# The lead-in of a fused attention and GLU block: weight loads on one queue, the first copy ahead of the second Sqrt, two more tiles transposed by DMA, paced loads

## The chip, the cores and the metric

The kernel runs on one core of a Trainium2 chip. The metric is the device time of one execution in microseconds (us); several executions are timed and the median is quoted. All points in time inside an execution are counted from the start of the profile's span (its first instruction). "Granted clock" is the mean clock that TensorE was allowed, 1.0 being full.

## The reference

The input x has 2048 rows of 640 numbers (bf16). The parts that matter here:

```python
xn  = (x - mean(x)) / sqrt(var(x) + 1e-5)          # LN, row by row
qkv = xn @ wqkv                                    # 640 x 1920
o   = sliding_dilated_attention(q, k, v)           # 32 heads of 20, window 8, dilation 2
out = x + o @ wo + ((xn @ w_gate) * (xn @ w_up)) @ w_down
```

The kernel cuts the rows into 16 tiles of 128. Each tile is loaded, normalised on VectorE, and transposed, because TensorE needs xn with the 640 columns on the partitions. The projections to q and k then run tile by tile for tiles 0 to 3 (128-column matmuls), in pairs of tiles for 4 to 7 (256 columns: the "wide" projections), and four tiles at a time from tile 8 on (512 columns). After that TensorE has nothing but long runs of 512- and 320-column matmuls until the end.

## The kernel before

Every operation is recorded in program order by a small scheduler, which puts it on its engine's list and inserts the semaphore waits. So the order of the Python calls is the order on each engine.

The loads. SyncE ("sp") and ScalarE ("act") share the weights of q (group 0) and k (group 1):

```python
x_load(1, "act")
x_load(0)
for c in range(NCH):                     # NCH = 5 chunks of 128 rows
    wqkv_load(0, c, ("sp", "act")[c % 2])
x_load(2, "act")
x_load(3)
for c in range(NCH):
    wqkv_load(1, c, ("sp", "act")[c % 2])
for t in range(4, 8):
    x_load(t)
```

LN of one tile is spread over four helpers. Tiles 0 to 3 are transposed on TensorE (`ln_pe`) and copied out of PSUM (`ln_copy`); tiles 4 to 15 (`NTP = 4`) go through a DMA transpose on SyncE's queue, and each applied tile sends for the x eight tiles ahead:

```python
def ln_aggr(t):
    ...                                  # bn_aggr on VectorE
    if t >= 8:                           # 1/sqrt on GpSimd: an addition, then pow(-0.5)
        ...
        return
    op("act", ... ACT.Sqrt ...)          # on ScalarE; VectorE takes the reciprocal

def ln_apply(t):
    ...
    op("dve", ... (x - mean) * rstd ...)
    if t >= NTP:
        op("sp", lambda e: e.dma_start_transpose(o, xs), ...)
    if t + 8 < NT:
        x_load(t + 8)
    elif t == NT - 1:
        late_loads()

def ln_next(t):
    ln_stats_b(t); ln_aggr(t); ln_stats_a(t + 1); ln_apply(t)
```

Note the last function: VectorE takes half of the statistics of tile t+1 *before* it applies tile t. A late x of tile 5 therefore holds back tile 4.

## Time and profile before

| | before |
|---|---|
| median time | 255.28 us (3 runs, 255.06 to 255.30) |
| span of the profile | 253.7 us |
| TensorE busy | 249.7 us, 98% |
| first projection / tile 2 / wide / 512 columns start at | 6.72 / 13.98 / 19.57 / 30.48 us |
| DMA transposes of tiles 5, 7, 11 land at | 18.79, 22.95, 29.93 us |

Two lines of the profile page, from its parts 1 and 4 (busy time with its share of the span and the number of instructions; shares of the chain of work that ended last):

```profile
PE 249.7 (98%) x1573; PEld 149.3 (59%) x1573; DVE 216.5 (85%) x241; ACT 112.9 (45%) x202; POOL 47.0 (19%) x73
...
PE 95%; DMA 2%; DVE 1%; ACTq 0%; ACT 0%; issue 0%
```

TensorE (PE) is the bound, and all but about the first ten and the last two microseconds of the chain are its own work. The timeline of TensorE, from 5 to 40 us (columns: start, duration, engine, source line, operation, output<-inputs, shapes, count, and in brackets the idle time before and what ended it):

```profile
6.72 1.03 PE L468 MATMUL PS<-XNT,WQKV 128*128 128x128 bf16 x15 [0.18 <-ACT XNT L414]
...
10.34 0.45 PE L403 MATMUL PS<-IDENT,XNS 128*128 128x128 bf16 x5 [0.34 <-DVE XNS L389]
...
13.98 5.75 PE L457 MATMUL PS<-XNT,WQKV 128*128 128x128 bf16 x100
19.57 11.08 PE L475 MATMUL PS<-XNT,WQKV 128*128 128x256 bf16 x100
30.48 9.88 PE L442 MATMUL PS<-XNT,WQKV 128*128 128x512 bf16 x45
```

L403 is a transpose on TensorE, the others are projections. After 10.34 us no bracket stands on any of these lines: TensorE never waits again. So whatever it gains or loses before about 31 us goes into the span in full.

The timeline of SyncE's DMA queue in the same stretch. A line is the time that the queue was held by the issue of a transfer, not the transfer itself:

```profile
13.94 1.33 SPq L393 DMA_TRANSPOSE XNT<-XNS  x1
15.32 0.57 SPq L294 DMA_DIRECT2D XST<-in_A_x_dram  x1
15.93 1.21 SPq L393 DMA_TRANSPOSE XNT<-XNS  x1
...
21.44 0.58 SPq L294 DMA_DIRECT2D XST<-in_A_x_dram  x1
22.07 14.79 SPq L393 DMA_TRANSPOSE XNT<-XNS  x8
```

The issue of a transpose holds the queue for 1.21 us, that of an x load for 0.58. The queue has only four loads between its transposes and then eight transposes in a row, with pauses, as they wait for VectorE. Tile 11's lands at 29.93, and TensorE wants it at 30.48: the slack is 0.55 us. Tile 5's is 0.8 us, tile 7's about 2 us.

### The profile page before, as it was taken

What the parts mean: (1) busy time and instruction counts of PE and PEld (TensorE: products, weight loads), DVE (VectorE), ACT (ScalarE), POOL (GpSimd) and SP (SyncE); (2) the same over time, 40 slices, a digit from 0 to 9 for tenths busy, and PEclk for the clock granted to TensorE, in tenths of its full rate; (3) what the DMA queues carried; (4) which work ended last, traced back from release to release, by engine and by line L of the source; (5) the groups of instructions that cost most, each with busy time, mean ns of one, the idle gap of its engine ahead of it and who ended that gap; (6) DMA issues with size and microseconds to landing.
All of it is one profiled execution on the core that took longest, in us unless ns stands there. A gap on an engine that the chain in (4) does not pass through costs nothing.

```text
span 253.7 us, 3853 instructions
## 1 busy us (share of the span) xinstructions
PE 249.7 (98%) x1573; PEld 149.3 (59%) x1573; DVE 216.5 (85%) x241; ACT 112.9 (45%) x202; POOL 47.0 (19%) x73
## 2 busy tenths in 40 slices
PE   8999999999999999999999999999999999999996
PEld 3899955555554444444444447764444777777775
DVE  5896679999999994999999994899999999995221
ACT  3575557555555557555555553325555112211000
POOL 2003320113453252002232102120000112112000
PEclk9999999999999999999999999999999999999999
DMA  6959448967866546364469962393000042332311
GB/s 213 332 117 170 82 79 303 375 178 142 138 127 110 106 83 125 114 238 90 75 117 253 393 230 24 51 314 68 3 0 0 4 50 26 36 45 26 80 52 52
DMA packets 25665, 31.84 MB, mean 126 GB/s; under 512 B 10000, under 2 KB 22160, under 8 KB 25616
## 3 DMA queue, kind: packets, MB, share of 16 engines
q1 hardware_dynamic: 18448, 21.31, 26.7%
q0 software_dynamic: 6336, 9.31, 23.7%
q10 hardware_dynamic: 864, 0.98, 1.2%
q8 instruction: 12, 0.20, 0.3%
q14 instruction: 5, 0.04, 0.0%
HBM read 14.42 MB, written 4.59 MB: 75 GB/s over the span
## 4 chain that ended last, share of the span: by engine, by line
PE 95%; DMA 2%; DVE 1%; ACTq 0%; ACT 0%; issue 0%
PE PS L614 41%; PE PS L645 29%; PE PS L442 17%; PE PS L475 4%; PE PS L457 2%; DMA XST<-in_A_x_dram 2%; PE PS L468 1%; DVE STATS L358 0%; ACTq L294 0%; PE PS L403 0%; ACT L321 0%; DVE XNS L389 0%; DVE STATS L364 0%; DVE FOUT L654 0%; DVE MV L370 0%
## 5 line engine op out<-in xcount | busy, mean ns | idle before, releaser
L614 PE MATMUL PS<-XNT,WG 128*128 128x512 bf16 x240 | 59.6, 379 | 0.0
L614 PE MATMUL PS<-XNT,WU 128*128 128x512 bf16 x240 | 59.6, 379 | 0.0
L581 DVE TENSOR_TENSOR PVB<-VO,ATB 128x10240 f16<-128x10240 bf16 x8 | 43.9, 5489 | 0.2
L442 PE MATMUL PS<-XNT,WQKV 128*128 128x512 bf16 x200 | 43.3, 379 | 0.0
L645 PE MATMUL PS<-WD,HT 128*128 128x320 bf16 (+1 forms) x300 | 43.2, 294 | 0.0
L614 PEld LDWEIGHTS PS<-XNT,WU 128*128 128x128 bf16 x240 | 23.5, 98 | 28.3
L614 PEld LDWEIGHTS PS<-XNT,WG 128*128 128x128 bf16 x240 | 23.5, 98 | 28.2
L616 ACT ACTIVATE USX<-PS 128x512 bf16<-128x512 f32 x48 | 28.7, 597 | 22.6 <-PE PS L614 22.2
L645 PEld LDWEIGHTS PS<-WD,HT 128*128 128x128 bf16 x300 | 28.7, 98 | 10.9
L442 PEld LDWEIGHTS PS<-XNT,WQKV 128*128 128x128 bf16 x200 | 23.5, 118 | 19.4
L576 DVE TENSOR_TENSOR PVB<-PVB 128x5120 f16<-128x5120 f16 (+1 forms) x16 | 34.5, 2156 | 0.3
L509 POOL DMA_DIRECT2D LOG<-PE x24 | 22.5, 937 | 57.6 <-DMA LOG<-PE 57.4
L649 ACT ACTIVATE FACC<-PS 128x320 f16<-128x320 f32 x24 | 10.5, 437 | 41.9 <-PE PS L645 41.9
L616 ACT ACTIVATE HT<-PS 128x512 bf16<-128x512 f32 x36 | 21.5, 597 | 16.5 <-PE PS L614 16.5
L645 PE MATMUL PS<-WO,VO 128*128 128x320 bf16 (+1 forms) x165 | 27.1, 295 | 0.0
L660 POOL DMA_DIRECT2D out_dram<-FACC x12 | 10.4, 865 | 71.2 <-ACT FACC L649 71.2
L645 PEld LDWEIGHTS PS<-WO,VO 128*128 128x128 bf16 x165 | 15.9, 98 | 5.9
L498 DVE TENSOR_TENSOR TMP<-QH,KH 128x2048 f16<-128x2048 bf16 x16 | 19.1, 1218 | 0.0
L498 DVE TENSOR_TENSOR PP<-QH,KH 128x2048 f16<-128x2048 bf16 x16 | 18.9, 1218 | 0.0
L503 DVE TENSOR_TENSOR PP<-PP,TMP 128x4096 f16<-128x4096 f16 x8 | 18.3, 2291 | 0.2
L654 DVE TENSOR_TENSOR FOUT<-PS,XR 128x320 bf16<-128x320 f32 (+1 forms) x9 | 4.1, 455 | 15.8 <-PE PS L645 15.8
L449 ACT ACTIVATE VO<-PS 128x512 bf16<-128x512 f32 x20 | 11.9, 597 | 9.6 <-PE PS L442 9.6
(65 smaller groups left out, 227.8 us busy)
## 6 DMA issues: line engine op xcount, KB each, us to landing
PE<-PP POOLq DMA_DIRECT2D x8, 512.0 KB, 4.8
ATB<-LOG SPq DMA_DIRECT2D x8, 512.0 KB, 4.3
LOG<-PE POOLq DMA_DIRECT2D x24, 128.0 KB, 2.7
XST<-in_A_x_dram SPq DMA_DIRECT2D x14, 160.0 KB, 4.7
WG<-in_B_w_gate_dram SPq DMA_DIRECT2D x1, 1920.0 KB, 9.4
WU<-in_B_w_up_dram SPq DMA_DIRECT2D x1, 1920.0 KB, 16.1
WD<-in_B_w_down_dram SPq DMA_DIRECT2D x1, 1920.0 KB, 10.3
out_dram<-in_A_x_dram SPq DMA_DIRECT2D x1, 1920.0 KB, 10.1
```

The costliest lines, as they stand in the source:

```text
L442: op("pe", (lambda l, x, c: lambda e: e.matmul(PS[:, b, :], l, x, start=(c == 0), stop=(c == NCH - 1)))(l, x, c), r=[l, x], w=[PS[:, b, :] ...
L449: op("act", lambda e: e.activation(o, PS[:, b, :], ACT.Copy, scale=sc), r=[PS[:, b, :]], w=[o], name=f"pev{which}_{m}_{j}")
L498: return (1.22, lambda: op("dve", lambda e: e.tensor_tensor(o, qw, kw, ALU.mult), r=[q, k], w=[o], name=f"prod{h}_{p}_{c}"))
L503: (2.3, lambda: op("dve", lambda e: e.tensor_tensor(a, a, b, ALU.add), r=[a, b], w=[a], name=f"psum{h}_{p}")),
L509: op("pool", lambda e: e.dma_start(o, i, accum_op=ALU.add), r=[o, i], w=[o], dma=True, name=name)
L576: return lambda: op("dve", lambda e: e.tensor_tensor(o, x, y, ALU.add), r=[x, y], w=[o], name=f"{name}_{b}")
L581: lambda: op("dve", lambda e: e.tensor_tensor(PVB[:], vw, aw, ALU.mult), r=[v, a], w=[PVB[:]], name=f"pv_{b}")),
L614: op("pe", (lambda l, x, c: lambda e: e.matmul(PS[:, b, :], l, x, start=(c == 0), stop=(c == NCH - 1)))(l, x, c), r=[l, x], w=[PS[:, b, :] ...
L616: op("act", lambda e: e.activation(o, PS[:, b, :], ACT.Copy), r=[PS[:, b, :]], w=[o], name=f"guev{which}_{m}_{j}")
L645: op("pe", (lambda l, x, i, b: lambda e: e.matmul(PS[:, b, 0:wid], l, x, start=(i == 0), stop=(i == n - 1)))(l, x, i, b), r=[l, x], w=[PS[ ...
L649: op("act", (lambda o, b: lambda e: e.activation(o, PS[:, b, 0:wid], ACT.Copy))(o, b), r=[PS[:, b, :]], w=[o], name=f"fin{t}_{nb}")
L660: stores.append(op("pool", lambda e: e.dma_start(d, f, accum_op=ALU.add), r=[f, ("out",)], w=[("out", t)], dma=True, name=f"oacc{t}"))
```

## The change

The intent: start TensorE sooner and take work off it. The weights go to one queue, so that all loads come in one order and x2 lands earlier (before: at 7.93 us). The copy of tile 0 goes ahead of the second Sqrt on ScalarE. Tiles 2 and 3 are transposed by DMA, so TensorE is spared ten transposes. To keep their DMA transposes from queueing behind x loads, the loads are paced: only x0 to x4 go out at the start, the others after the transposes. Both projections of one tile run together, so that tile 3 is wanted later. Not in the title, but in the diff: 1/sqrt of tiles 8 to 15 goes from GpSimd to ScalarE.

```diff
-    NTP = 4
+    NTP = 2
@@ the loads
     for c in range(NCH):
-        wqkv_load(0, c, ("sp", "act")[c % 2])
-    x_load(2, "act")
+        wqkv_load(0, c)
+    x_load(2)
     x_load(3)
     for c in range(NCH):
-        wqkv_load(1, c, ("sp", "act")[c % 2])
-    for t in range(4, 8):
-        x_load(t)
+        wqkv_load(1, c)
+    x_load(4)
@@ ln_aggr, ln_apply
-        if t >= 8:
-            (1/sqrt on GpSimd: cut)
-            return
...
-        if t + 8 < NT:
-            x_load(t + 8)
-        elif t == NT - 1:
+        ahead = {2: (5, 6), 3: (7, 8)}.get(t, (t + 5,) if t > 3 else ())
+        for u in ahead:
+            if u < NT:
+                x_load(u)
+        if t == NT - 1:
             late_loads()
@@ the lead-in
     ln_pe(0)
+    ln_copy(0, "act")
     ln_stats_b(1)
     ln_aggr(1)
-    ln_copy(0)
+    ln_copy(0, "dve")
@@ tr(t)
-        ln_pe(t)
-        ln_copy(t)
+        if t < NTP:
+            ln_pe(t)
+            ln_copy(t)
@@ the projections of tiles 0 to 3
-        for which in (0, 1):
-            for t in (t0, t0 + 1):
+        for which, t in ((0, 0), (0, 1), (1, 0), (1, 1)) if t0 == 0 else ((0, 2), (1, 2), (0, 3), (1, 3)):
...
-                    at = {(0, 0): (3, lambda: tr(1)), (0, 1): (4, lambda: tr(2)), (1, 1): (2, lambda: tr(3))}
+                    at = {(0, 0): (4, lambda: tr(1)), (1, 0): (3, lambda: tr(2)), (1, 1): (4, lambda: tr(3))}
```

More of the change, by code (lines that the diff above doesn't have):

```diff
@@ L284, in build_kernel @@
     EPSC = sb("EPSC", [128, 16], FP32)
-    NEGH = sb("NEGH", [128, 16], FP32)
     IDENT = sb("IDENT", [128, 128])
@@ L304, in build_kernel @@
     op("pool", lambda e: e.memset(VO[:, :, 0:VP], 0.0), w=[VO[:, :, 0:VP]], name="vpad")
-    op("pool", lambda e: e.memset(NEGH[:], -0.5), w=[NEGH[:]], name="negh")
     op("pool", lambda e: e.memset(MASK[:], 0.0), w=[MASK[:]], name="mask0")
@@ L370, in ln_aggr @@
         op("dve", lambda e: e.bn_aggr(mv, st), r=[st, ("stb", t)], w=[mv], name=f"bnag{t}")
-        if t >= 8:
-            rstd = SD[:, t, 1:2]
-            op("pool", lambda e: e.tensor_scalar(sd, mv[:, 1:2], EPS, None, op0=ALU.add), r=[mv], w=[("sd", t)], name=f"sd{t}")
-            op("pool", lambda e: e.tensor_tensor(rstd, sd, NEGH[:, 0:1], ALU.pow), r=[("sd", t), NEGH[:]], w=[("rstd", t)],
-               name=f"rstd{t}")
-            return
         op("act", lambda e: e.activation(sd, mv[:, 1:2], ACT.Sqrt, bias=EPSC[:, 0:1]), r=[mv, EPSC[:]], w=[("sd", t)],
@@ L384, in ln_apply @@
         sd, rstd = SD[:, t, 0:1], SD[:, t, 1:2]
-        if t < 8:
-            op("dve", lambda e: e.reciprocal(rstd, sd), r=[("sd", t)], w=[("rstd", t)], name=f"rstd{t}")
+        op("dve", lambda e: e.reciprocal(rstd, sd), r=[("sd", t)], w=[("rstd", t)], name=f"rstd{t}")
         for c0, c1 in ((0, 2 * 128), (2 * 128, D)) if t == 0 else ((0, D),):
@@ L403, in ln_pe, with ln_copy @@
             op("pe", (lambda o, i: lambda e: e.transpose(o, i, IDENT[:]))(o, i), r=[i, IDENT[:]], w=[o], name=f"tr{t}_{c}")
-    def ln_copy(t):
+    def ln_copy(t, only=None):
         parts = ((("act", 0, 2), ("dve", 2, NCH)), (("dve", 0, 2), ("act", 2, NCH)), (("act", 0, NCH),),
@@ L408, in ln_copy @@
         for eng, c0, c1 in parts:
+            if only is not None and eng != only:
+                continue
             o = XNT[:, c0:c1, t * TS:(t + 1) * TS]
@@ L709, in build_kernel @@
             bank_ring[:] = [5, 6, 0, 7, 2, 3, 4, 1]
-        for which in (0, 1):
-            for t in (t0, t0 + 1):
+        for which, t in ((0, 0), (0, 1), (1, 0), (1, 1)) if t0 == 0 else ((0, 2), (1, 2), (0, 3), (1, 3)):
+            if True:
                 b = bank()
```

## The prediction

> **What bounds the kernel now.** TensorE. On the profile page it is busy 249.7 of 253.7 us (98%), and 95% of the chain that ended last is its own. The timeline shows no gap in its matmuls from 10.34 us to 251.4 us, so only the lead-in can change the time: an advance there that still stands when the wide projections (pairs of tiles) start at 19.57 us, and the 512-column ones at 30.48 us, passes through whole.
>
> **What is to be won, by the timeline.**
> - The first copy of tile 0 waits on ScalarE behind the second Sqrt (6.10, copy at 6.30), though its two transposes were done near 5.5. Moved ahead, the first projection starts when the two filler matmuls have streamed, near 6.2 instead of 6.72: 0.5 us.
> - Gap of 0.26 us at 8.69 (copy behind tile 2's statistics; x2 landed at 7.93) and of 0.5 us before 10.34. With all loads in one order x2 is eighth. Loads landed every 0.5 to 0.58 us in this trace, so about 6.5 to 7.1. The Trainium skill, "DMA: Bandwidth & Descriptors" (Issuing engines are not separate DMA queues), says that several issuers only save sequencer time; here SyncE issues one load per 0.45 us, about the landing rate, so I expect no loss of bandwidth.
> - Ten TensorE transposes (two fives of 0.28 us issue time): 0.56 us.
>
> Projections of tiles 0 and 1 should thus end near 12.2 us instead of 13.98: about 1.75 us.
>
> **What it adds.** A DMA transpose holds SyncE's queue for 1.2 us and lands 2.6 to 4.2 us after issue. VectorE applies tile 2 at about 9.3 to 9.7, so its transpose lands at 12.4 to 13.3: a wait of 0.2 to 1 us at once. Then the paced loads: x5 goes out only after that transpose, at 11.0, and lands near 13.8 (2.8 us in this trace). VectorE runs the statistics of tile 5 before it applies tile 4, so it stands idle for some 1.5 us; the application of tile 4 moves from 13.46 to about 14.5, of tile 5 from 15.14 to 16.1. With x9 before it on the queue, tile 5's transpose is issued at 16.8 (before 15.93) and lands at 19.5 to 20.5. The wide projections need it; TensorE would be ready at 18.1 to 18.8. So it waits about 1 us and starts at 19.4 to 20.5, against 19.57. A load after every transpose (1.87 us a tile on SyncE) also puts tile 11's transpose at about 27.9, landing 30.5 to 31.2.
>
> Sqrt for tiles 8 to 15 returns to ScalarE (0.29 us, GpSimd 0.8), so LN ends 2 us sooner; nothing waits for that.
>
> **Sum.** 1.75 us is gained by the end of tile 1, and nearly all given back at tiles 2, 5 and perhaps 11. My chain gives -0.2 to +0.9 us; the latencies, read from loads under other contention, are uncertain by half a microsecond each, and a luckier x5 keeps up to 1 us of gain. I say 255.2 us, range 254.2 to 256.3. Faster by over 2%: 1%, within: 98%, slower: 1%.
>
> **What would show it.** Right: first projection near 6.2, tile 1 done near 12.2, TensorE idle before tile 2's and above all before the first wide projection, put down to a DMA transpose; VectorE idle near 12 to 14 waiting for x. Wrong on the cost: wide projections start near 18 us and the time is near 253.7. Wrong on the gain: x2 still lands near 8.
>
> **What would make it wrong.** Transposes queued behind loads landing over 4 us late; late K weights; the idle time lowering the granted clock; qk products starting earlier and colliding with the weight loads.

## The result, and the profile after

The change is slower, by about 1.5%: 258.75 us median of 6 runs (257.68 to 260.78) against 255.22 (255.06 to 255.34). The ratio is 1.0146, with a 95% interval of 1.0107 to 1.0184. The prediction of 255.2 (254.2 to 256.3) was wrong. Note the spread too: before stays within 0.3 us, the change scatters over 3 us.

The traced execution was the fastest of the six (257.68 us, span 255.4). The same two lines of its page:

```profile
PE 248.9 (97%) x1563; PEld 148.5 (58%) x1563; DVE 217.9 (85%) x249; ACT 112.9 (44%) x208; POOL 41.1 (16%) x56
...
PE 86%; DVE 6%; DMA 4%; SPq 1%; issue 1%; ACT 0%
```

TensorE has 0.8 us less to do, but its share of the chain fell from 95% to 86%: VectorE, DMA landings and SyncE's queue are now on it. TensorE's timeline:

```profile
6.12 1.28 PE L462 MATMUL PS<-XNT,WQKV 128*128 128x128 bf16 x20
...
8.16 4.38 PE L462 MATMUL PS<-XNT,WQKV 128*128 128x128 bf16 x75 [0.20 <-DVE XNT L406]
13.26 5.78 PE L451 MATMUL PS<-XNT,WQKV 128*128 128x128 bf16 x100 [0.72 <-DMA XNT<-XNS]
19.82 5.66 PE L469 MATMUL PS<-XNT,WQKV 128*128 128x256 bf16 x50 [0.78 <-DMA XNT<-XNS]
26.23 5.65 PE L469 MATMUL PS<-XNT,WQKV 128*128 128x256 bf16 x50 [0.76 <-DMA XNT<-XNS]
32.13 8.15 PE L436 MATMUL PS<-XNT,WQKV 128*128 128x512 bf16 x37 [0.25 <-ACT SD L368]
```

The first projection starts 0.6 us earlier, and tiles 0 and 1 are done near 12.4 instead of 13.98. Then TensorE waits for DMA transposes: for tile 2, for tile 5 (first wide projection), for tile 7 (second one), and for tile 11 (its transpose landed at 32.04; the profile names the Sqrt that ended just before). The 512-column projections start at 32.13 instead of 30.48, 1.65 us later, and the span is 1.7 us longer.

SyncE's queue:

```profile
16.85 1.21 SPq L383 DMA_TRANSPOSE XNT<-XNS  x1
18.10 0.58 SPq L293 DMA_DIRECT2D XST<-in_A_x_dram  x1
18.72 2.17 SPq L383 DMA_TRANSPOSE XNT<-XNS  x1
20.94 0.58 SPq L293 DMA_DIRECT2D XST<-in_A_x_dram  x1
21.56 1.21 SPq L383 DMA_TRANSPOSE XNT<-XNS  x1
...
28.53 0.58 SPq L293 DMA_DIRECT2D XST<-in_A_x_dram  x1
29.15 7.40 SPq L383 DMA_TRANSPOSE XNT<-XNS  x5
```

Load and transpose now take turns up to tile 11, 1.87 us a tile (1.21 and 0.58, and two pauses of 0.04), without a break. One transpose, tile 6's, held the queue for 2.17 us. Tile 11's goes out at 29.15 (before: 27.30) and lands at 32.04 (before: 29.93).

Two more traces of the same kernel were taken later (runs e13 and e14). The starts, in us:

| | before | after | e13 | e14 |
|---|---|---|---|---|
| first projection | 6.72 | 6.12 | 6.04 | 6.04 |
| tile 2 | 13.98 | 13.26 | 13.34 | 13.47 |
| first wide | 19.57 | 19.82 | 20.32 | 19.84 |
| tile 11's transpose issued / landed | 27.30 / 29.93 | 29.15 / 32.04 | 29.44 / 32.37 | 29.30 / 32.28 |
| 512 columns | 30.48 | 32.13 | 32.68 | 32.59 |
| span | 253.7 | 255.4 | 255.7 | 255.6 |
| time minus span | 1.83 | 2.28 | 2.28 | 2.32 |

So e13 and e14 show the same loss as the first trace; they did not catch one of the slower runs, for which they were taken. The last row of the table is a surprise of its own: 0.46 us of the difference lies outside the profile's span. It is taken up by e16 to e18.

### The profile page after: what moved, and what is told of

It reads as the page before. It is cut to its first block, busy times and chain, and to the rows that moved or that the text cites. A ratio compares the mean times of both kernels' runs of the same rounds, so it can differ in the third digit from the quotient of the medians.

```text
span 255.4 us, 3830 instructions
## 1 busy us (share of the span) xinstructions
PE 248.9 (97%) x1563; PEld 148.5 (58%) x1563; DVE 217.9 (85%) x249; ACT 112.9 (44%) x208; POOL 41.1 (16%) x56
## 4 chain that ended last, share of the span: by engine, by line
PE 86%; DVE 6%; DMA 4%; SPq 1%; issue 1%; ACT 0%
PE PS L608 41%; PE PS L639 29%; PE PS L436 17%; DMA XST<-in_A_x_dram 4%; DVE STATS L361 2%; DVE XNS L379 2%; DVE STATS L355 2%; SPq L293 1%; DVE MV L367 1%; DVE SD L376 1%; SPq L383 0%; DVE FOUT L648 0%; ACT SD L368 0%; DVE XNT L406 0%
## 5 line engine op out<-in xcount | busy, mean ns | idle before, releaser
L503 POOL DMA_DIRECT2D LOG<-PE x24 | 21.7, 920 | 59.4 <-DMA LOG<-PE 59.4
L648 DVE TENSOR_TENSOR FOUT<-PS,XR 128x320 bf16<-128x320 f32 (+1 forms) x9 | 4.1, 455 | 15.5 <-PE PS L639 15.5
```

Source lines behind the costliest of these rows:

```text
L503: op("pool", lambda e: e.dma_start(o, i, accum_op=ALU.add), r=[o, i], w=[o], dma=True, name=name)
```

## The experiments

The theories. A: the paced loads, taking turns with the transposes on SyncE's queue, make the transposes of tiles 5, 7 and 11 late. B: the DMA transposes of tiles 2 and 3 are what costs. C: Sqrt of tiles 8 to 15 on ScalarE holds up the copies out of PSUM there and so TensorE. D: a long wait of TensorE cuts its clock. E: instruction fetches delay the transposes in flight. F, about the time outside the span, came late. "Before" ran beside every group, on the same chip: 255.4 to 255.7 us.

### e1 to e4: one part undone at a time

e1, only the pacing undone:

```diff
-    x_load(4)
+    for t in range(4, 8):
+        x_load(t)
...
-        ahead = {2: (5, 6), 3: (7, 8)}.get(t, (t + 5,) if t > 3 else ())
+        ahead = (t + 8,)
```

> The change with only the pacing undone: x4 to x7 go out at the start, each later load eight tiles ahead. Theory A (paced loads put tiles 5, 7 and 11 on a chain of SyncE issues and DMA landings): tile 2's transpose lands later, near 13.8 us, behind more loads, but VectorE no longer waits for x5, the first wide projection starts near 19.4 instead of 19.8 and the 512-column projections near 30.5 instead of 32.1; time 255.0 to 255.8 us. Rival B (the DMA transposes of tiles 2 and 3 are what costs): stays above 257. Rival C (Sqrt of tiles 8 to 15 on ScalarE ties LN to the PSUM copies): stays above 257.

e2, only tiles 2 and 3 back on TensorE:

```diff
-    NTP = 2
+    NTP = 4
```

> The change with only tiles 2 and 3 back on TensorE transposes. Theory A: x5 and x6 need not wait behind a transpose any more and land near 12.5, tile 2 costs TensorE no wait; first wide projection near 18.5, but SyncE still alternates load and transpose up to tile 10, so tile 11 lands near 29.6 to 30.5 and the 512-column projections start at about 29.8 to 30.6; time 254.4 to 255.4 us. Rival B: as good as before or better, 254.0 to 254.5, with no wait left on the later tiles. Rival C: above 257.

e3, both edits together:

> Both undone: left are the one queue for the weights, the earlier first copy, the order of projections and Sqrt on ScalarE throughout. Theory A: nothing holds TensorE after tile 1; 512-column projections start near 29.3, time 253.8 to 254.4 us, better than before. Rival C: above 257, as Sqrt on ScalarE is still there.

e4, the change with 1/sqrt of tiles 8 to 15 on GpSimd again (the lines of `ln_aggr` and the reciprocal's `if t < 8` of before put back):

> The change with 1/sqrt of tiles 8 to 15 back on GpSimd. Theory A: no tile 8 to 15 is limited by it, so the same as the change, 257.5 to 259.5 us, or up to 0.5 us slower, as LN needs 2.1 us a tile instead of 1.66. Rival C (ScalarE's Sqrt holds the PSUM copies and TensorE's banks): back to 255 to 256.

| | median (range), us | before beside it | ratio [95%] |
|---|---|---|---|
| e1 pacing undone | 258.82 (257.15 to 260.03) | 255.65 | 1.0121 [1.0068, 1.0174] |
| e2 tiles 2, 3 on TensorE | 256.64 (256.09 to 259.18) | 255.65 | 1.0061 [1.0009, 1.0112] |
| e3 both | 255.67 (255.29 to 256.67) | 255.65 | 1.0009 [0.9983, 1.0035] |
| e4 1/sqrt on GpSimd | 259.06 (258.65 to 262.02) | 255.65 | 1.0161 [1.0102, 1.0219] |

Theory C falls with e4: the time does not come back, not even in its two runs at a full clock (258.65 and 258.66). Theory A alone falls with e1. Without pacing, tile 2's transpose is issued at 9.97 but lands at 15.04, because five more x loads are ahead of it, and TensorE's timeline reads:

```profile
15.08 7.41 PE L452 MATMUL PS<-XNT,WQKV 128*128 128x128 bf16 x100 [2.35 <-DMA XNT<-XNS]
22.32 11.08 PE L470 MATMUL PS<-XNT,WQKV 128*128 128x256 bf16 x100
```

The wait is 2.35 us. And look at the duration: the 100 matmuls that take 5.78 us in the change take 7.41 here. The granted clock fell after the wait, to 0.50 for 3.41 us. The view by stretches shows it (the stretch and its length, busy times of the five engines, then the clock, the DMA share and GB/s):

```profile
15.51:18.92 3.41, 3.41 (x36) 3.41 (x35) 1.85 (x6) 0.78 (x2) 0.00 (x0) 0.50 0.85 188
```

Three of e1's four runs have such a cut (mean clock 0.993). The one at a full clock took 257.15 us, less than any full-clock run of the change (257.68 to 259.36), but still 1.5 us more than before. So the equal medians of e1 and the change hide two things: at a full clock undoing the pacing wins something (by one run), and the longer wait at tile 2 that it brings cuts the clock more often. The pacing does what it was made for, at tile 2, and takes away later what it gave.

e2 recovers 2.2 us of the 3.2 that separate the change (258.83 in e9) from before, and e3 all of it; neither theory had forecast e2's time, which is above both of its ranges. So B is the larger part. Once the two transposes are gone the pacing has nothing to protect, and the turns on the queue (A) are worth the other 1 us: tile 11's transpose went out at 28.99 us in e2's trace and at 26.97 in e3's. My expected gain for e3 (253.8 to 254.4) did not come. Its trace shows the 512-column projections at about the same time as before; about 0.5 us of its lead was lost waiting for tile 7, whose transpose landed at 24.85 instead of 22.95. Another half is outside the span: e3's four spans (253.0 to 254.4 us) are a little shorter than those of before beside it (253.4 to 254.2), but 2.3 us are lost outside them instead of 1.8 (see e16).

In e2's trace, its slowest run (259.18), the clock shows again:

```profile
13.35 5.75 PE L451 MATMUL PS<-XNT,WQKV 128*128 128x128 bf16 x100
21.05 12.78 PE L469 MATMUL PS<-XNT,WQKV 128*128 128x256 bf16 x100 [1.95 <-DMA XNT<-XNS]
```

The wide projections, 11.08 us at a full clock, took 12.78 after a wait of 1.95 us. The mean clock of that run is 0.993; the other three runs have 1.0 and lie at 256.1 to 256.7.

### e5: does a long wait cut the clock?

```diff
+    def filler(n):            # n matmuls of 512 zero columns into the bank that comes next
+        ...
+                if (which, t) == (0, 2):
+                    filler(4)
...
+            if g == 0:
+                filler({4: 5, 6: 4}[t0])
```

> The change, with 4, 5 and 4 filler matmuls (0.22 us each) on TensorE just before the three places where it waits for DMA transposes. Theory D (a wait of TensorE near 2 us or longer halves its clock for some us and costs another 1.6 us; that makes the upper half of the change's times): mean granted clock 1.0 in every run, the slow runs are gone, all runs 257.4 to 258.8 us, median near 258.0. Rival (the spread comes from DMA landings alone): spread as before, 257.5 to 261, median 0.3 to 0.6 us later than the change's 258.75.

Measured: 259.68 us (258.64 to 260.01), ratio 1.0154. Half a miss. The clock was 1.0 in all four runs (lowest 0.999), and the range is 1.4 us instead of 3. But the median did not fall. In its trace tile 2's transpose held the queue for 2.60 us, tile 5's landed at 22.3, and TensorE waited 1.81 us on top of the fillers. The test was not clean, though: tile 7's transpose landed at 25.26, long before TensorE wanted it, so the four fillers there (27.80 to 28.67) cost 0.87 us for nothing. Without them the trace would stand at about 258.8 (an estimate), the change's median. What settles it is the change itself: ten of its eleven runs (e9's 681 us aside) have a clock of 0.999 or 1.0, and these lie between 257.68 and 259.36. So the clock explains the highest times, not the middle.

Over all traces (without e9 and e12, see there), a wait of TensorE for a transpose was followed by slow matmuls in five of seven cases where it lasted 1.95 us or more (e1 2.35, e2 1.95, e4 2.74, e6 2.00, e7 3.77; not in e7's first, 2.00, nor in e8, 2.35), and in none where it was 1.86 us or less. Each cut lasted 3.41 us at half the clock and so cost 1.6 to 1.7 us; one such cut in some 256 us makes the mean clock of 0.993, and two make the 0.987 of the slowest runs of e4 and e8 (an estimate: neither was traced). The Trainium skill, "TensorE: Matmul & The Clock Gate" (Part 1), says that the clock falls to half after an idle window of about 3.4 us, and that this window runs freely. The traces fit this in that the same wait, 2.00 us, is punished in e6 and not in e7; but here four of the five waits that were punished lasted only 1.95 to 2.74 us, and the measurement decides.

### e6: does an instruction fetch delay the transposes?

The 2.17 us of tile 6's transpose and the landing of tile 7's, 4.6 us after its issue, had no cause in the kernel. But the DMA view has a queue of kind "instruction" with one packet near each. The DMA view of the change, narrowed to 19.0 to 19.5 us and to 24.0 to 24.5 us (queue, kind: packets, MB, share of 16 engines in that half microsecond):

```profile
q8 instruction: 1, 0.02, 16.8%
```

```profile
q14 instruction: 1, 0.01, 9.7%
```

The first packet, 16 KB, took 16.8% of 16 engines for 0.5 us: 1.34 us on one engine. To test it, the fetch was moved:

```diff
-    warm(10)                  # 10 warm-up matmuls of 512 columns
+    warm(36, 128)             # 36 of 128 columns: as long, but 52 instructions more
```

> The change, with the 10 warm-up matmuls of 512 columns replaced by 36 of 128 columns: as long, but 52 more TensorE instructions ahead, so that each later 16 KB fetch of the instruction queue comes 26 matmuls, some 1.5 to 3 us, earlier. Theory E (an instruction fetch delays the transposes in flight by 1 to 2 us): the fetch at 19.0 us moves to about 17.3, tile 5's transpose (issued 16.85) then lands near 21 to 22 instead of 19.75, tile 6's issue is no longer the long one, TensorE waits 2 us or more before the first wide projection; median 259.5 to 261 us. Rival (the long landings come from the load beside each transpose): the long ones stay at tiles 6 to 8, time as the change, 257.7 to 259.4.

Measured: 258.36 us (257.79 to 258.97), ratio 1.0111. The size was a miss, the mechanism a hit. The fetch moved from 19.10 to 16.40 us, and SyncE's queue of this run reads:

```profile
14.83 1.21 SPq L383 DMA_TRANSPOSE XNT<-XNS  x1
16.08 0.58 SPq L293 DMA_DIRECT2D XST<-in_A_x_dram  x1
16.71 2.09 SPq L383 DMA_TRANSPOSE XNT<-XNS  x1
18.84 0.58 SPq L293 DMA_DIRECT2D XST<-in_A_x_dram  x1
19.47 1.21 SPq L383 DMA_TRANSPOSE XNT<-XNS  x1
```

The long hold went from tile 6 (now the 1.21 at 19.47) to tile 5 (2.09), and the long flight, 4.4 us, to tile 4. TensorE waited 2.00 us before the first wide projection, and its clock was cut in three of the four runs. The time did not rise because the earlier fetch moved too (10.58 to 9.81), and tile 2's transpose, which it used to hit, landed at 12.4 instead of 13.2: there was no wait at tile 2.

All traces together say the same. Take the 194 DMA transposes issued after 13 us in the 16 traces whose x loads are all on hardware queues. The 93 with no instruction packet during their flight landed 2.6 to 3.3 us after issue (median 2.8). The 101 with one had a median of 3.5 and went up to 4.9; all 52 flights over 3.45 us are among them. Every transpose that held the queue for more than 1.45 us had a fetch beside it. The Trainium skill, "DMA: Bandwidth & Descriptors" (Queues, rings and completion order), says that a DMA engine takes turns between its queues packet by packet. A 16 KB packet of 0.9 to 1.9 us would then hold back whatever a transpose has queued on the same engine. That this is the way it happens is argued, not shown; and a fetch is no certain delay, as 28 of the 101 landed within 3.0 us all the same.

### e7 and e8: the x loads on GpSimd's queue

e7, the change with x9 to x15 issued by GpSimd, so that SyncE has only transposes from tile 4 on:

```diff
-                x_load(u)
+                x_load(u, "pool" if u > 8 else "sp")
```

> The change, with x9 to x15 loaded from GpSimd's queue, so that SyncE issues transposes alone from tile 4 on. Theory A (load and transpose take turns on SyncE's queue at 1.87 us a tile): tile 5's transpose is issued near 16.6, tile 7's near 20.0 instead of 21.56, tile 11's near 26.6 instead of 29.15; the waits before the second wide projection and the 512-column ones (0.95 and 0.3 us) go, the one at tile 5 stays; 256.0 to 257.4 us. If the bytes in flight and not the queue's turns are what delays them: 257.7 to 259.4.

e8, an attempt at a better kernel: e3, with x8 to x15 on GpSimd's queue and `ln_stats_a(2)` after the copy of tile 1:

> An attempt at a better kernel: early first copy, weights on one queue and projections tile by tile are kept; tiles 2 and 3 go back to TensorE, x4 to x7 go out at the start, x8 to x15 from GpSimd's queue, and the statistics of tile 2 follow the copy of tile 1 on VectorE. TensorE then waits at neither tile 1 nor tiles 5, 7, 11: first wide projection near 18.4 us, 512-column ones near 29.3 to 29.8, 254.0 to 254.8 us against 255.3 to 255.7 before. If a fetch still lands late transposes on TensorE: 255.2 to 256.2.

Both missed by far: e7 260.21 us (258.55 to 261.61), ratio 1.0180; e8 258.83 (257.50 to 262.49), ratio 1.0111; e8's 262.49 counts as a slow run, and without it the median is 258.17. The issues do come earlier (tile 7's at 20.76), but the landings do not. The DMA view of e7 for tile 7's issue alone (last column: us from issue to landing):

```profile
XNT<-XNS SPq DMA_TRANSPOSE x1, 7.1
```

Tiles 4 to 9 took 5.3, 6.5, 6.3, 7.1, 5.6 and 4.0 us; tiles 10 to 14, when the loads were over, 2.6 each. So, for the landings, loads from GpSimd's queue in flight beside a transpose are far worse than loads between the transposes on SyncE's own queue, where both land in about 2.9 us; why, these runs don't show, and ScalarE's queue was not tried. In time the difference is smaller: three of e7's four runs have a cut clock (0.993), and the fourth took 258.55 us, about as long as the change. The queue's turns were not the only price of the paced loads, but they were the cheaper way to pay it.

### e9, e13, e14: the change again

> The change itself once more, on the chip of the runs beside it, for a second trace and its spread: 257.5 to 261 us. Every theory expects the waits of TensorE at tile 2 and before the first wide projection; if an instruction fetch is what delays transposes, the transposes in flight at the fetch near 19 and near 24 us are again the ones over 3.5 us; if a wait near 2 us cuts the clock, a run with a mean clock of 0.993 has one and is over 1.5 us longer than the fastest.

> The change, one more trace, for a typical run (its first trace was its fastest run of six). If it is DMA landings behind instruction fetches that make 258.8 out of 257.7 at a full clock: one of tiles 2 to 7 lands 1 us or more later than in the first trace, with a fetch inside its flight, and TensorE's wait grows by as much; nothing after 35 us differs.

> As the run before: a third trace. The same two expectations; if the extra time is instead after the lead-in, the 512-column projections start near 32.1 us in both and the end still differs.

e9: 258.83 us (three runs of 258.29 to 258.87, ratio 1.0125); its fourth, the traced execution, took 681 us, with TensorE slow from end to end (512-column matmuls of 835 ns instead of 379), and is left aside. e13 and e14 gave 257.98 and 257.92 us. TensorE in e14:

```profile
13.47 5.78 PE L451 MATMUL PS<-XNT,WQKV 128*128 128x128 bf16 x100 [0.84 <-DMA XNT<-XNS]
19.84 11.11 PE L469 MATMUL PS<-XNT,WQKV 128*128 128x256 bf16 x100 [0.59 <-DMA XNT<-XNS]
32.59 7.72 PE L436 MATMUL PS<-XNT,WQKV 128*128 128x512 bf16 x35 [1.64 <-ACT QH L477]
```

The time is lost in the lead-in, as in the first trace, but at other places: no wait at tile 7, 1.64 us at tile 11. (That one of tiles 2 to 7 would land later and TensorE's wait there grow was expected and did not come: tile 6's landed at 23.58 instead of 22.55, but nothing waited for it.) The weight load of that first 512-column matmul started at 32.34, right after tile 11's landing at 32.28, so the transpose is what mattered; the ScalarE copy that the bracket names ended 0.1 us later. In all three traces tile 11's issue is where the sum of the queue puts it: from tile 4's at 14.97, 15.75 and 15.21, seven turns of 1.87 us give 13.1, and the rest (1.1, 0.6 and 1.0 us) is what a fetch held the queue (tile 6's transpose 0.96 over its usual time; x11's load 0.57; x11's load 0.96). In e13 a fetch had also held the queue at tile 2's transpose (2.25 us instead of 1.32), and from there its tile 4 is late.

### e10: the DMA transposes alone, on the kernel before

```diff
-    NTP = 4
+    NTP = 2
...
-        ln_pe(t)
-        ln_copy(t)
+        if t < NTP:
+            ln_pe(t)
+            ln_copy(t)
```

> The kernel before, with only tiles 2 and 3 transposed by DMA. If these transposes are what costs (theory B): tile 2's lands at 14 to 15.5 us behind x loads, TensorE waits 1 to 2.5 us before tile 2 and its clock may be cut; 256.8 to 259.5 us. If the pacing or Sqrt on ScalarE costs (A, C): within 0.5 us of before.

Measured: 256.51 us (256.10 to 259.13), ratio 1.0062 [1.0025, 1.0099]. Theory B again: this part alone costs 1 us, and 3.7 us in the one run whose clock was cut (0.993). Tile 2's transpose was issued at 10.32 and landed at 14.6, and TensorE, which had saved ten transposes, lost more than it saved:

```profile
14.64 5.78 PE L457 MATMUL PS<-XNT,WQKV 128*128 128x128 bf16 x100 [1.55 <-DMA XNT<-XNS]
```

### e11: the one queue alone, on the kernel before

```diff
-        wqkv_load(0, c, ("sp", "act")[c % 2])
-    x_load(2, "act")
+        wqkv_load(0, c)
+    x_load(2)
...
-        wqkv_load(1, c, ("sp", "act")[c % 2])
+        wqkv_load(1, c)
```

> The kernel before, with only the weights and x2 moved to SyncE's queue. x2 lands at 7.4 to 7.9 instead of 7.93; the gaps of TensorE at 8.69 and 10.34 us shrink by 0.2 to 0.6 us in all and nothing later moves: 254.7 to 255.3 us. If weights on one queue arrive later than TensorE wants them: slower, 255.5 to 256.5.

Measured: 255.08 us (255.03 to 255.37) against 255.47, ratio 0.9987 [0.9974, 1.0000]. This is the best kernel, by 0.13%: small, as expected, and just at the edge of what the runs resolve. x2 landed at 7.39 instead of 7.93:

```profile
9.83 0.45 PE L403 MATMUL PS<-IDENT,XNS 128*128 128x128 bf16 x5 [0.20 <-DVE XNS L389]
...
13.49 5.75 PE L457 MATMUL PS<-XNT,WQKV 128*128 128x128 bf16 x100
19.08 11.08 PE L475 MATMUL PS<-XNT,WQKV 128*128 128x256 bf16 x100
30.04 10.31 PE L442 MATMUL PS<-XNT,WQKV 128*128 128x512 bf16 x47
```

Half a microsecond is won at tile 2 and kept to the end. No more could be: tile 11's transpose landed at 29.95, so the slack there is now 0.1 us. The skill's word on queues, cited in the prediction, holds here roughly: the last weights of k landed at 10.43 us in the change and 10.81 in e11 with one queue, and at 10.19 with two, and the timeline shows no matmul waiting for them.

### e12, e15, e17: two more attempts at a better kernel

e12 and e15 are one kernel: e3, with `ln_stats_a(2)` after the copy of tile 1, and with the transposes of tiles 1 and 3 one chunk of five matmuls earlier in TensorE's order.

> Second attempt at a better kernel: early first copy, one queue, projections tile by tile, Sqrt on ScalarE are kept; tiles 2 and 3 on TensorE, loads eight tiles ahead, statistics of tile 2 after the copy of tile 1, tile 1's transposes after 15 matmuls. Tile 1 done near 12.9 us, first wide projection near 18.4 (19.57 before); fetches still delay tiles 6 and 7 and give back some 0.5 us: 254.6 to 255.4 us against 255.5.

> The second attempt at a better kernel once more (its trace fell into a state with a clock of 0.756): 254.9 to 257.3 us. If late landings of tiles 6 and 7 take its gain: TensorE is done with tile 1 near 12.9 us, starts the first wide projection near 18.4, and waits 0.5 to 2 us before the second.

e12: one execution of 330 us, its traced one, had a granted clock of 0.756 and is left aside; the other five lie at 254.87 to 257.25, median 256.58, ratio 1.0036 [1.0011, 1.0062]: a little slower than before, and above the 254.6 to 255.4 expected. e15: 256.48.

e17 is e3 with eight idle GpSimd instructions (see e16):

> A third attempt at a better kernel: run e3 (tiles 2 and 3 on TensorE, loads eight tiles ahead; the early copy, the one queue, the order of projections and Sqrt on ScalarE kept) with the eight idle GpSimd instructions. Theory F: the time exceeds the span by 1.8 us, so 255.2 us median (254.8 to 256.2), 0.45 us better than e3 and level with the queue-only kernel. Rival: 255.7 us as e3.

e17: 256.20 us (254.50 to 256.42), ratio 1.0017 [0.9995, 1.0039], against an expected median of 255.2. Its six runs are two groups, 254.5 and 254.9, and 256.15 to 256.42. The two traces, of two kernels that differ a little, suggest why such a kernel has two times. TensorE in e15, and then in e17's fastest run:

```profile
12.85 5.75 PE L452 MATMUL PS<-XNT,WQKV 128*128 128x128 bf16 x100
20.00 11.11 PE L470 MATMUL PS<-XNT,WQKV 128*128 128x256 bf16 x100 [1.41 <-DMA XNT<-XNS]
31.17 9.01 PE L437 MATMUL PS<-XNT,WQKV 128*128 128x512 bf16 x41
```

```profile
12.97 5.75 PE L455 MATMUL PS<-XNT,WQKV 128*128 128x128 bf16 x100
18.55 11.08 PE L473 MATMUL PS<-XNT,WQKV 128*128 128x256 bf16 x100
29.47 10.74 PE L440 MATMUL PS<-XNT,WQKV 128*128 128x512 bf16 x49
```

In both, tile 5's transpose went out at 15.5 to 15.6 us. In e15 an instruction fetch came at 17.58 and the transpose landed at 19.96; in e17 it came at 17.70 and the transpose landed at 18.25. So TensorE waits 1.41 us in the one and not in the other, for fetches that are 0.1 us apart (0.2 counted from the issue). That this small shift makes the difference is argued, not shown. The slow group of e17 was not traced itself; that it is the same event is an inference from e15.

### e16 and e18: the time outside the span

Theory F: 2.28 us instead of 1.82 outside the span comes from GpSimd having nothing to do between 2.5 and 33 us.

e16, the change with one idle GpSimd addition for each of tiles 8 to 15:

```diff
+        if t >= 8:
+            op("pool", lambda e: e.tensor_scalar(scr, mv[:, 1:2], EPS, None, op0=ALU.add), ...)
```

> The change with eight idle GpSimd instructions more (a scalar addition of 0.2 us for each of tiles 8 to 15, whose result nobody reads), between about 20 and 35 us. Of every run of a kernel in which GpSimd worked in that stretch, the time exceeds the profile's span by 1.8 us, of every run of the others by 2.28 us. Theory F (that stretch of GpSimd without work costs 0.46 us outside the span): 1.8 us here, 258.3 us instead of 258.8. Rival (it hangs on the pow, on another op or on the number of instructions, 73 against 56): 2.28 us.

e18, the change with 17 tiny memsets on GpSimd at the very start:

> The change with 17 more GpSimd instructions (tiny memsets) at the very start and none later, so that it has as many as before. Theory F (idle stretch): time minus span stays 2.28 us. Rival (number of instructions): 1.8 us. The time itself is that of the change, 257.5 to 260 us.

Both bring it back. Time minus span is 1.77 to 1.86 us in e16's four runs and 1.78 in e18. So F, the idle stretch, falls: in e18 GpSimd has nothing to do from 5.0 to 34.9 us, nearly as in the change (2.5 to 35.6). Of the explanations named, the number of GpSimd instructions is left. The change and e3 have 56 and lose 2.28; before has 73, e18 73, e16, e17 and e8 64, e7 63, and all of these lie at about 1.8 (1.75 to 1.99). Where on the way to the end this time passes, the profile does not show. In the time, e16 gave 258.17 us (257.86 to 258.78), ratio 1.0104; e18 gave 256.68 in its one run, faster than any run of the change itself, with no late tile 7 and a fetch at 18.9.

## Why the prediction was wrong, point by point

- *TensorE is the bound and only the lead-in counts.* Right. In nearly every trace the shift at 30 to 33 us is, within 0.2 us (0.4 in e10), the shift of the span.
- *First projection near 6.2, x2 at 6.5 to 7.1, tile 1 done near 12.2.* Right but for x2 (7.39): 6.12, and about 12.4.
- *A wait of 0.2 to 1 us at tile 2; the first wide projection at 19.4 to 20.5.* Right: about 0.7 to 0.8 us, and 19.8 to 20.3.
- *VectorE waits for x5.* Right: the timeline shows it idle for 1.36 us before the statistics of tile 5, until 13.91.
- *"A load after every transpose (1.87 us a tile on SyncE) also puts tile 11's transpose at about 27.9, landing 30.5 to 31.2."* This is the step that failed. The turns were sized right, 1.87 us each, and tile 5 stood where the forecast had it (16.8; 16.85 in the first trace). But the sum had no term for the queue being held: between tiles 4 and 11 the fetches add 0.6 to 1.1 us to it, and in e13 another 0.9 at tile 2. Tile 11 was issued at 29.15 to 29.44 and landed at 32.0 to 32.4. The forecast then took this tile only for a possible extra ("and perhaps 11") and summed to -0.2 to +0.9 us; the traces have +1.65 to +2.2 in the lead-in. In the first trace tile 7 was late as well (a flight of 4.62 us beside a fetch), which the forecast did not have at all.
- *The sum had no term for what lies outside the span.* The diff also takes 17 instructions off GpSimd, to which the prediction gave no cost. They are worth 0.46 us (e16, e18). Together with the lead-in this makes up the first trace (257.68 us, 2.15 above the traced execution of before, 255.53); the 1.1 us from there to the median of 258.75 is not in any trace of the change.
- *"The idle time lowering the granted clock"* was named as a risk and left out of the range. It is real: 1.6 to 1.7 us in the runs that it hits (the 260.78 of the change has a clock of 0.993). It makes the top of the scatter, not the median: of the change's runs, this one alone had a clock under 0.999.
- *Which part costs.* The prediction blamed the pacing above all. The runs say: the DMA transposes of tiles 2 and 3 first (e10 alone +1.0 us; taking them out, e2, -2.2), the pacing second (e3 against e2, -1.0), and undoing the pacing alone is no cure (e1: the same median, 257.15 at a full clock). The costs don't add up one by one: the same two DMA transposes cost 1.0 us on the kernel before (e10) and 3.2 on e3 (e1 against e3, about half of it the clock), where TensorE reaches tile 2 earlier and the transpose lands later (15.04 us against 14.59). The one queue is a gain (e11).

What stays open: the runs of the change with a full clock and a span of 256.4 to 257.1 were not caught in a trace, so that they too are late landings is an inference from the traces with spans up to 256.0 (e16). The early copy and the order of projections were not run alone. Why fewer GpSimd instructions cost time outside the span is not known.

## What to carry to other kernels

A DMA transpose that nobody waited for cost nothing here, and one with half a microsecond of slack was a gamble: before you move work from a saturated engine to a queue, subtract the landing time *with its spread* from the moment the result is wanted, and count how long each issue holds the queue. Removing 0.6 us of work from the busiest engine was worth nothing here, where the next thing to arrive was bound by a queue; as long as tile 11's transpose lands where it did before, its slack of 0.55 us is the whole gain to be had. It need not stay there: in e17's fastest run (254.50 us), with Sqrt on ScalarE and without pacing, tile 11's transpose landed at 28.85 instead of 29.93 and the 512-column projections started at 29.47, 1.0 us earlier. The prediction said of this earlier end of LN that "nothing waits for that"; once the lead-in is shorter, TensorE does. When a kernel gets slower and also scatters more, look for the slack that used to hide a jitter.

## What the Trainium skill lacked or had wrong

- "DMA: Bandwidth & Descriptors", and no other page: what instruction fetches do to other transfers. Here DMA transposes with a fetch of 8 or 16 KB during their flight landed in 3.5 us (median), at most 4.9, against 2.8 without, and the hold of the issuing queue rose from 1.21 to as much as 2.9 us (e3).
- The same page: nothing on how plain loads from GpSimd's queue delay DMA transposes on SyncE's: 4.0 to 7.1 us to landing in e7, against 2.6 when the loads were over.
- "Advanced Engine Details and Errata" (X-Bar Transpose (TRN2)) says that transposes by DMA are as fast as regular ones. For the landing the traces agree (2.6 to 3.3 us with no fetch in flight, and 2.4 to 3.2 for an x load of the same size, both with a median of 2.8). What the issue costs the page does not say: here a transpose held the queue for 1.21 us and an x load for 0.58, and the turns of the two set when tile 11's transpose went out.
- "TensorE: Matmul & The Clock Gate" (Part 1): the clock is said to fall after about 3.4 us of idleness; here it fell after five of seven waits of 1.95 us or more, and four of these five were shorter than that (1.95 to 2.74 us). Each time it stayed at half for 3.41 us, at a cost of 1.6 to 1.7 us.
- No page has it: with 56 GpSimd instructions the time exceeded the profile's span by 2.28 us, with 63 or more by about 1.8.
